# All rows through GpSimd's casting queue: retention followed by a token and channel mixer, on one core

## The chip, the core and the metric

The kernel runs on one core of one Trainium2 chip. The metric is device time in microseconds (us) of one execution, the median of several. A run's state is fast unless it lies over 1.5% above the fastest of the same kernel; only fast runs enter a ratio. A ratio is the mean time of one kernel's fast runs over the mean of the other's fast runs of the same rounds, so it is not quite the ratio of the medians quoted beside it. In the profiles PE is the matrix engine, PEld its weight loads, DVE is VectorE, ACT is ScalarE, POOL is GpSimd and SP is SyncE; each has its own instruction queue.

## The reference

Four batches, eight heads, 768 steps, 64 columns per head. A decayed recurrence over the steps is followed by a mixer over tokens and a mixer over channels (d_tok 256, d_ch 1536):

```python
state = gamma[None, :, None, None] * state + np.einsum('bhd,bhe->bhde', k[:, :, t], v[:, :, t])
y[:, :, t] = scale * np.einsum('bhd,bhde->bhe', q[:, :, t], state)
...
h = np.maximum(xt @ w_tok1, 0.0) @ w_tok2
u = x + h.transpose(0, 2, 1)
h2 = np.maximum(u @ w_ch1, 0.0) @ w_ch2
return (u + h2).astype(np.float32)
```

Inputs and output are f32. The kernel computes in f16 and works in chunks of 128 steps and pairs of heads.

## The kernel before

The kernel doesn't run in the order in which it is written. Every piece of work becomes an `Op` with the engines that may do it and a cost for each. While the program is built, `arrange()` plays the ops through with these costs, picks an engine and a moment for each, and the result is a fixed order for each engine. The plan doesn't exist at run time any more. There, each engine takes its instructions in the planned order and waits at each one for whatever it really depends on. A wrong estimate in the plan therefore never gives a wrong result: it makes an engine stand still at an instruction while others that are ready wait behind it.

For each engine `w[0]` that may do an op, `arrange()` asks when the op could start on it.

```python
for w in op.ways:
    start = max(base, free[w[0]])
    for d in op.deps:
        if d.eng == w[0] and (d.dma or d.eng == "PE"):
            continue
        start = max(start, d.end + (30 if d.eng == w[0] else SEM) + op.guard)
    done = start + w[2] + (300 if w[0] == "DVE" else 0)
    if pick is None or done < pick[0]:
        pick = (done, start, w)
```

For a transfer, `d.end` is the planned landing, worked out by `wires()` from packets and a constant `LAND` per queue. The `continue` skips the wait when the thing waited for was issued by the same engine and is a transfer (`d.dma`).

Rows of k, q and v, for a pair of heads of one batch, come in three ways (cut):

```python
# load(b, p): k and q as f32 by SP's hardware queue, v cast to f16 by GpSimd's software queue
nc.sync.dma_start(out=t, in_=r.rearrange("h (c p) d -> p (h c) d", p=P))        # k, q
nc.gpsimd.dma_start(out=tile_of(s, [P, 2, NC, D], F16), in_=...)                # v
# front(b, p): q is cast and put in the layout of two heads side by side
    ql = parts(emit, dict(POOL=(770, 860), ACT=(780, 860)), [qd], Q, QF, (slice(0, 2),))
# turn(): batches 2 and 3 are transposed by a DMA from SP's queue, batches 0 and 1 by PE
```

`front(b, p)` (recurrence and token mixer of a pair) and `back(b)` (channel mixer of a batch) of different batches interleave. The channel mixer needs no new rows, so it can fill PE while rows come in, if the plan puts it there.

Of the kernel before, what the change touches and what calls it, by code (L numbers as in the profile page):

```python
# [10 lines left out]
FP = mybir.dt.float32  # L11
F16 = mybir.dt.float16
# [5 lines left out]
def kernel(  # L18
# [11 lines left out]
    nc = tc.nc  # L30
    B, H, S, D = q.shape
    P = 128
    NC = S // P
    HC = NC // 2
# [13 lines left out]
    ctx.enter_context(tc.manual_schedule())  # L48


    BUFS = dict(kf=4, qf=4, k16=3, q16=3, v16=6, kT=4, qT=4, U=2, r16=3, am=8, X=3, x16=5, h1=5, u16=3,
                uT=3, h2=2, o=4)
    BANKS = dict(first=range(0, 7), front=range(0, 5), back=range(5, 8), fill=range(7, 8))
    SEM = 80
    XB = 2
# [19 lines left out]
            ops.append(self)  # L75

    GEN = dict(SP=20, ACT=20)
    FIRST = dict(SP=600, POOL=1300, ACT=600)
    LAND = dict(SP=800, POOL=1000, ACT=1500)

    def wires(order):
# [125 lines left out]
    def tile_of(slot, shape, dtype):  # L207
        if slot.bank is not None:
            slot.tile = ps.tile(shape, dtype, name=f"bank{slot.bank}", bufs=1)
        else:  # L210
            slot.tile = sb.tile(shape, dtype, name=slot.tag, bufs=BUFS[slot.tag])
        return slot.tile

    def act(n, scaled=False):
        t = 186 + (93 if scaled else 0) + 5 * n // 6
        return t - 60, t + 20

    def dve(n, per=1.04):
        return int(140 + n * per), int(170 + n * per)
# [4 lines left out]
    def one(eng, cost, emit):  # L224
        return [(eng, cost[0], cost[1], emit)]
# [11 lines left out]
    ident16 = const_p.tile([P, P], F16, name="ident16")  # L237
# [4 lines left out]
    r16 = [const_p.tile([P, NC - 1, P], F16, name=f"r16_{i}") for i in range(NR)]  # L242
# [7 lines left out]
    def emit():  # L250
        nc.gpsimd.iota(itp, pattern=[[0, 1]], base=-MID, channel_multiplier=1,
                       allow_small_or_imprecise_dtypes=True)
# [16 lines left out]
    g_op = prep("ACT", 500, emit, [lgs_op])  # L269

    ident_op = prep("POOL", 560, lambda: make_identity(nc, ident16), prio=(0, -1, 1))
# [11 lines left out]
    wt1 = const_p.tile([P, NC, DT], F16, name="wt1")  # L283
    wt2 = const_p.tile([P, NJ, S], F16, name="wt2")
    NW = 3
    FW = NF // NW
    wc1 = [const_p.tile([P, NP, FW * P], F16, name=f"wc1_{i}") for i in range(NW)]
    wc2 = [const_p.tile([P, FW, C], F16, name=f"wc2_{i}") for i in range(NW)]
    wops = {}
    queue = []  # L290

    def request(prio, cost, emit, dma, takes=()):
        o = Op(prio, [("POOL", cost, cost, emit)], [], takes, dma=dma,
               after=queue[-6:-5], behind=queue[-1] if queue else None)
        queue.append(o)
        return o

    def weight(key, n, ns, dst, src):
        def emit():
            nc.gpsimd.dma_start(out=dst, in_=src.rearrange("(i p) j -> p i j", p=P))  # L300
        wops[key] = request((0, 0, 9), 850, emit, (n, ns))


    casts_of = {(b, p): [] for b in range(B) for p in range(NP)}
# [3 lines left out]
    first_of = {}  # L308
    rcount = [0]

    rows = []

    def load(b, p):
        got = []
        for tag, src in (("kf", k), ("qf", q)):
            s = Slot(tag)

            def emit(s=s, src=src, tag=tag):
                t = tile_of(s, [P, 2, NC, D], FP)
                r = src[b, 2 * p:2 * p + 2]  # L320
                if b < XB and tag == "qf":
                    nc.sync.dma_start(out=t.rearrange("p h (f i) d -> p h f (i d)", f=2),  # L322
                                      in_=r.rearrange("h (f p i) d -> p h f (i d)", f=2, p=P))
                else:
                    nc.sync.dma_start(out=t, in_=r.rearrange("h (c p) d -> p (h c) d", p=P))  # L325
            o = Op((0, b, p), [("SP", 100, 100, emit)], [], [s], dma=(32, 36) if b < XB and tag == "qf" else (96, 17),
                   after=rows[-4:-3], behind=rows[-1] if rows else None)
            rows.append(o)
            got.append((s, o))
        s = Slot("v16")  # L330

        def emit(s=s):
            nc.gpsimd.dma_start(out=tile_of(s, [P, 2, NC, D], F16),  # L333
                                in_=v[b, 2 * p:2 * p + 2].rearrange("h (c p) d -> p (h c) d", p=P))
        got.append((s, request((0, b, p), 1040, emit, (96, 15), [s])))
        loads[b, p] = got

    def front(b, p):
        first, last = b == 0, b == 0 and p == NP - 1
# [3 lines left out]
        def op(ways, deps=(), takes=(), uses=(), late=0, behind=None):  # L343
            n[0] += 1
            pe = ways[0][0] == "PE"
            pr = (late, b, n[0], p) if first else (late, b, p, n[0])
            return Op(pr, ways, deps, takes, uses, guard=200 if pe and not first else 0, behind=behind)

        def parts(emit, costs, deps, slot, src, steps):

            got = []
            for st in steps:
                def put(e, st=st):
                    emit(e, st)
                got.append(op(either(put, **costs), deps, [] if got else [slot],
                              ([slot] if got else []) + [src], behind=got[-1] if got else None))
            return got
# [4 lines left out]
        X, UT = Xs[b], UTs[b]  # L362
        pc = slice(p * P, (p + 1) * P)
        (KF, kd), (QF, qd), (V, vl) = loads[b, p]
        K, Q = Slot("k16"), Slot("q16")
# [5 lines left out]
        def emit(e, js):  # L371
            t = opened(K, [P, NC, 2, D], F16)
            for j in js:
# [2 lines left out]
                    nc.scalar.activation(t[:, :, j], KF.tile[:, j], AF.Copy, scale=gk[:, h:h + 1])  # L376
                else:
                    nc.vector.tensor_scalar(t[:, :, j], KF.tile[:, j], gk[:, h:h + 1], None, ALU.mult)
        kl = parts(emit, dict(ACT=(540, 610), DVE=(490, 540)), [kd, g_op], K, KF, ([0], [1]))

        def emit(e, js):
            t = opened(Q, [P, NC, 2, D], F16).rearrange("p c h d -> p h c d")[:, js]
# [1 line left out]
                nc.scalar.copy(t, QF.tile[:, js])  # L384
            else:
                (nc.vector if e == "DVE" else nc.gpsimd).tensor_copy(t, QF.tile[:, js])  # L386
        if last:
            ql = parts(emit, dict(POOL=(400, 510), ACT=(440, 510), DVE=(490, 540)), [qd], Q, QF,
                       (slice(0, 1), slice(1, 2)))
        elif first:  # L390
            ql = parts(emit, dict(POOL=(770, 860)), [qd], Q, QF, (slice(0, 2),))
        else:
            ql = parts(emit, dict(POOL=(770, 860), ACT=(780, 860)), [qd], Q, QF, (slice(0, 2),))
        casts_of[b, p] += ql

        def flat(t):
            return t.rearrange("p c h d -> p (c h d)")
# [1 line left out]
        def turn(src, dst, dep):  # L399
            if b >= XB:  # L400
                def emit():
                    t = tile_of(dst, [P, S], F16)
                    nc.sync.dma_start_transpose(out=t.rearrange("d (c t) -> d c t", t=P),
                                                in_=flat(src.tile))
                o = Op((0, b, p, 0), [("SP", 100, 100, emit)], dep, [dst], [src], dma=(48, 24))
                return [o, o]
            T = Slot(FA)

            def emit():
                tp = tile_of(T, [P, 1024], F16)  # L410
                for c in range(NC):
                    nc.tensor.transpose(tp[:, c * P:(c + 1) * P], src.tile[:, c].rearrange("p h d -> p (h d)"), ident16)  # L412
            t = op(one("PE", (340, 500), emit), dep + [ident_op], [T], [src])

            def emit(e, hs):
                d, o = opened(dst, [P, S], F16), T.tile[:, :S]
                if dst is QT:
                    d = d.rearrange("d (f p i) -> d f p i", f=2, i=HC)[:, hs]
                    o = o.rearrange("d (f i p) -> d f p i", f=2, i=HC)[:, hs]
                else:  # L420
                    d = d.rearrange("d (f t) -> d f t", f=2)[:, hs]
                    o = o.rearrange("d (f t) -> d f t", f=2)[:, hs]
                (nc.scalar.copy if e == "ACT" else nc.vector.tensor_copy)(d, o)
            per = 1.04 if dst is QT else 0.54
            if last:
                return parts(emit, dict(ACT=act(S // 2), DVE=dve(S // 2, per)), [t], dst, T,
                             (slice(0, 1), slice(1, 2)))
            return 2 * parts(emit, dict(ACT=act(S), DVE=dve(S, per)), [t], dst, T, (slice(0, 2),))
        kt = turn(K, KT, kl)
        qt = turn(Q, QT, ql)  # L430

        two_before = y_done.get(b * NP + p - 2)
        ST, US, RS = Slot(FA), Slot("U"), Slot("r16")
# [277 lines left out]

    for p in range(NP):
        load(0, p)
    weight("t1", 48, 60, wt1, moe_w_tok1)
    weight("t2", 16, 134, wt2, moe_w_tok2)
    for i in range(NW):
        weight(("c1", i), 32, 97, wc1[i], moe_w_ch1[:, i * FW * P:(i + 1) * FW * P])
    for i in range(NW):
        weight(("c2", i), 32, 97, wc2[i], moe_w_ch2[i * FW * P:(i + 1) * FW * P])
    for b in range(1, B):  # L720
        for p in range(NP):
            load(b, p)
# [8 lines left out]
            front(b, p)  # L731
    for b in range(B):
        back(b)
    for key, o in (("t1", casts_of[0, 2][0]), (("c1", 0), casts_of[0, 3][-1])):
        wops[key].deps.append(o)
    best = None
    for turn in range(8):
        order = arrange()
# [50 lines left out]
```

## Time and profile before

216.36 us, median of three runs (215.75 to 217.79). The profiled span is 215.9 us.

| | before |
|---|---|
| PE busy | 199.0 us, of it 12.5 us warm-up on zeros |
| PE not busy (span less busy) | 16.9 us |
| GpSimd busy | 55.9 us |
| DMA engines at 90% or more | until slice 24 of 40, about 130 us |
| last block of PE, two channel mixers without a gap | from 150 us, 62 us long |

A row of the page's second part is read slice by slice: one slice is 5.4 us, a 9 is at least 90% busy. PE is the limit after 130 us and would be before, if rows and what is made of them came in time. The lines themselves stand in the prediction.

### The profile page before, as it was taken

What the parts mean: (1) busy time and instruction counts of PE and PEld (TensorE: products, weight loads), DVE (VectorE), ACT (ScalarE), POOL (GpSimd) and SP (SyncE); (2) the same over time, 40 slices, a digit from 0 to 9 for tenths busy, and PEclk for the clock granted to TensorE, in tenths of its full rate; (3) what the DMA queues carried; (4) which work ended last, traced back from release to release, by engine and by line L of the source; (5) the groups of instructions that cost most, each with busy time, mean ns of one, the idle gap of its engine ahead of it and who ended that gap; (6) DMA issues with size and microseconds to landing.
All of it is one profiled execution on the core that took longest, in us unless ns stands there. A gap on an engine that the chain in (4) does not pass through costs nothing.

```text
span 215.9 us, 4706 instructions
## 1 busy us (share of the span) xinstructions
PE 199.0 (92%) x1893; PEld 123.0 (57%) x1893; DVE 103.7 (48%) x269; ACT 113.1 (52%) x244; POOL 55.9 (26%) x90
## 2 busy tenths in 40 slices
PE   7698799996999999859998699999999999999993
PEld 3465588552367765426665576676645645545541
DVE  6288947402579986118788368874012012012021
ACT  4468996772088964248361677542721712703700
POOL 8225862211016545004332134343000000000000
PEclk9969999999699999999999699999999999999999
DMA  7999999999999999999999998254202112012012
GB/s 156 197 179 263 221 211 219 200 203 181 188 185 226 169 136 162 243 259 173 163 216 159 207 158 165 49 85 108 66 5 105 38 45 101 3 49 99 0 52 99
DMA packets 93207, 30.99 MB, mean 144 GB/s; under 512 B 81920, under 2 KB 90112, under 8 KB 93184
## 3 DMA queue, kind: packets, MB, share of 16 engines
q1 hardware_dynamic: 60672, 17.31, 50.8%
q0 software_dynamic: 29056, 7.08, 35.6%
q10 hardware_dynamic: 3456, 6.29, 8.3%
q8 instruction: 15, 0.25, 0.5%
q14 instruction: 8, 0.07, 0.1%
HBM read 26.74 MB, written 6.29 MB: 153 GB/s over the span
## 4 chain that ended last, share of the span: by engine, by line
PE 69%; DMA 18%; SPq 5%; ACT 3%; DVE 2%; issue 1%; ACTq 0%; POOL 0%
PE bank L695 27%; PE bank L668 25%; DMA v<-in_v_dram 11%; DMA kf<-in_k_dram 5%; PE bank L599 4%; PE bank L548 4%; SPq L322 3%; PE bank L507 2%; PE bank L482 2%; DMA qf<-in_q_dram 2%; PE bank L504 2%; PE bank L439 2%; SPq L325 1%; ACT X L520 1%; DVE am L490 1%; PE bank L412 1%
## 5 line engine op out<-in xcount | busy, mean ns | idle before, releaser
L668 PE MATMUL bank<-uT,wc 128*128 128x384 f16 x384 | 69.4, 327 | 5.0 <-ACT h L682 5.0
L682 ACT ACTIVATE h<-bank 128x384 f16<-128x384 f32 x96 | 46.1, 491 | 49.9 <-DVE o L703 24.0
L695 PE MATMUL bank<-wc,h 128*128 128x512 f16 x288 | 69.3, 386 | 0.1
L668 PEld LDWEIGHTS <-wc 128*128 128x128 f16 x384 | 35.7, 98 | 27.9 <-issue 5.8
L703 DVE TENSOR_TENSOR o<-X,bank 128x512 f32<-128x512 f32 x24 | 16.5, 688 | 62.0 <-PE bank L695 61.9
L695 PEld LDWEIGHTS <-h 128*128 128x128 f16 x288 | 26.9, 99 | 29.1 <-issue 2.0
L490 DVE TENSOR_TENSOR am<-bank,mask 128x384 f16<-128x384 f32 x64 | 32.1, 550 | 21.4 <-PE bank L482 21.3
L333 POOL DMA_DIRECT2D v<-in_v_dram x16 | 16.7, 1043 | 20.9 <-PE bank L507 10.9
L520 ACT ACTIVATE X<-bank,gy 128x192 f32<-128x192 f32 x50 | 18.0, 419 | 7.1 <-PE bank L507 6.9
L537 POOL CAST x<-X 128x384 f16<-128x384 f32 x23 | 12.0, 521 | 30.2 <-ACT X L520 16.4
L607 DVE TENSOR_TENSOR X<-X,bank 128x384 f32<-128x384 f32 x32 | 16.3, 550 | 5.8 <-PE bank L599 5.4
L615 POOL CAST u<-X 128x384 f16<-128x384 f32 x23 | 11.3, 509 | 28.7 <-DVE X L607 25.6
L451 DVE SCALAR_TENSOR_TENSOR U<-U,gp,bank 128x64 f32<-128x64 f32 x64 | 17.8, 278 | 1.5
L507 PE MATMUL bank<-v,am 128*128 128x64 f16 x192 | 15.0, 197 | 0.5 <-DVE am L490 0.4
L376 ACT ACTIVATE k<-kf,gk 128x384 f16<-128x384 f32 x22 | 12.8, 609 | 3.4 <-DMA kf<-in_k_dram 3.3
L599 PE MATMUL bank<-h,wt 128*128 128x128 f16 x192 | 14.0, 225 | 0.7 <-ACT h L556 0.7
L507 PEld LDWEIGHTS <-am 128*128 128x128 f16 x192 | 12.9, 101 | 2.8 <-DVE am L490 0.8
L462 ACT ACTIVATE r<-U 64x320 f16<-64x320 f32 x26 | 12.1, 467 | 3.5 <-DVE U L451 3.1
L599 PEld LDWEIGHTS <-wt 128*128 128x128 f16 x192 | 12.2, 101 | 2.8 <-issue 0.9
L386 POOL CAST q<-qf 128x768 f16<-128x768 f32 (+1 forms) x12 | 9.8, 815 | 15.2 <-DMA qf<-in_q_dram 15.2
L756 PE MATMUL bank<-zero 128*128 128x384 f16 x53 | 12.5, 382 | 1.2 <-DVE zero L248 1.2
L548 PE MATMUL bank<-x,wt 128*128 128x128 f16 x192 | 13.4, 219 | 0.2 <-DMA wt<-in_moe_w_tok_dram 0.2
(56 smaller groups left out, 154.0 us busy)
## 6 DMA issues: line engine op xcount, KB each, us to landing
kf<-in_k_dram SPq DMA_DIRECT2D x16, 384.0 KB, 9.3
qf<-in_q_dram SPq DMA_DIRECT2D x16, 384.0 KB, 9.8
out_dram<-o ACTq DMA_DIRECT2D x24, 256.0 KB, 2.0
v<-in_v_dram POOLq DMA_DIRECT2D x16, 192.0 KB, 14.6
wc<-in_moe_w_ch_dram POOLq DMA_DIRECT2D x6, 512.0 KB, 16.5
wt<-in_moe_w_tok_dram POOLq DMA_DIRECT2D x2, 384.0 KB, 7.6
kT<-k SPq DMA_TRANSPOSE x8, 6.1
qT<-q SPq DMA_TRANSPOSE x8, 6.2
```

What stands on the lines that cost most here:

```text
L333: nc.gpsimd.dma_start(out=tile_of(s, [P, 2, NC, D], F16), in_=v[b, 2 * p:2 * p + 2].rearrange("h (c p) d -> p (h c) d", p=P))
L451: nc.vector.scalar_tensor_tensor(U[:, c], U[:, c - 1], gp[:, p:p + 1], o, ALU.mult, ALU.add)
L490: nc.vector.tensor_tensor(am, src, m, ALU.mult)
L507: nc.tensor.matmul(o[:, j * D:(j + 1) * D], AM[2 * hf + j].tile[:, i], V.tile[:, j, c], start=(c == 0), stop=(c == 0 or j == 1))
L520: nc.scalar.mul(X.tile[:, half(hf), h * D:(h + 1) * D], yv[:, :, j * D:(j + 1) * D], gy[:, h:h + 1])
L548: nc.tensor.matmul(acc[:, jt * P:(jt + 1) * P], wt1[:, i, jt * P:(jt + 1) * P], X16.tile[:, i], start=(i == 0), stop=(i == NC - 1))
L599: nc.tensor.matmul(acc[:, i * P:(i + 1) * P], wt2[:, jt, t], H1.tile[:, jt], start=(jt == 0), stop=(jt == NJ - 1))
L607: nc.vector.tensor_tensor(xo, xo, T2.tile[:, :HC * P].rearrange("p (i d) -> p i d", d=P), ALU.add)
L668: nc.tensor.matmul(acc[:, :SH], w[:, ct, (ft % FW) * P:(ft % FW + 1) * P], UT.tile[:, ct, sh * SH:(sh + 1) * SH], start=(ct == 0), stop=(c ...
L682: nc.scalar.activation(H2.tile[:, ft], A.tile[:, :SH], AF.Relu)
L695: nc.tensor.matmul(A.tile, H2.tile[:, ft, i * P:(i + 1) * P], wc2[ft // FW][:, ft % FW], start=(ft == 0), stop=(ft == NF - 1))
L703: nc.vector.tensor_tensor(o, X.tile[:, sh * HC + i], A.tile, ALU.add)
```

## The change

The intent: let the casting queue of GpSimd bring all rows as f16, so that the f32 casts of q go away and SP's queue is free for transposes; order that queue as it is needed (rows of the first batch, weights, the rest); and for batches 0 and 1 let PE turn q straight from the loaded tile, one head at a time, so that q isn't copied there at all. In batches 2 and 3 q is still copied into the layout of two heads, now from f16 to f16, and VectorE is added to the engines that may do it.

```diff
-    BUFS = dict(kf=4, qf=4, k16=3, q16=3, v16=6, ...
+    BUFS = dict(kf=6, qf=6, k16=3, q16=3, v16=8, ...
-    FIRST = dict(SP=600, POOL=1300, ACT=600)
+    FIRST = dict(SP=600, POOL=1700, ACT=600)
...
-               after=queue[-6:-5], behind=queue[-1] if queue else None)
+               after=queue[-8:-7], behind=queue[-1] if queue else None)
...
-        for tag, src in (("kf", k), ("qf", q)):
+        for tag, src in (("kf", k), ("qf", q), ("v16", v)):
...
+            def emit(s=s, src=src):
+                nc.gpsimd.dma_start(out=tile_of(s, [P, 2, NC, D], F16),
+                                    in_=src[b, 2 * p:2 * p + 2].rearrange("h (c p) d -> p (h c) d", p=P))
...
-        else:
-            ql = parts(emit, dict(POOL=(770, 860), ACT=(780, 860)), [qd], Q, QF, (slice(0, 2),))
+        if b < XB:
+            ql = [qd]
+        else:
+            ql = parts(emit, dict(POOL=(770, 860), ACT=(780, 860), DVE=(500, 550)), [qd], Q, QF, (slice(0, 2),))
...
+                    if src is QF:
+                        for j in range(2):
+                            nc.tensor.transpose(o[j * D:(j + 1) * D], src.tile[:, j, c], ident16)
```

Cut: costs of single ops in the plan, the place of the first two requests in its order, the waits of two weight requests for casts that no longer exist, and the plain eviction of the turned q, which the new layout allows.

More of the change, by code (lines that the diff above doesn't have):

```diff
@@ L48 @@
     ctx.enter_context(tc.manual_schedule())
-    BUFS = dict(kf=4, qf=4, k16=3, q16=3, v16=6, kT=4, qT=4, U=2, r16=3, am=8, X=3, x16=5, h1=5, u16=3,
+    BUFS = dict(kf=6, qf=6, k16=3, q16=3, v16=8, kT=4, qT=4, U=2, r16=3, am=8, X=3, x16=5, h1=5, u16=3,
                 uT=3, h2=2, o=4)
@@ L309 @@
     rcount = [0]
-    rows = []
     def load(b, p):
         got = []
-        for tag, src in (("kf", k), ("qf", q)):
+        for tag, src in (("kf", k), ("qf", q), ("v16", v)):
             s = Slot(tag)
-            def emit(s=s, src=src, tag=tag):
-                t = tile_of(s, [P, 2, NC, D], FP)
-                r = src[b, 2 * p:2 * p + 2]
-                if b < XB and tag == "qf":
-                    nc.sync.dma_start(out=t.rearrange("p h (f i) d -> p h f (i d)", f=2),
-                                      in_=r.rearrange("h (f p i) d -> p h f (i d)", f=2, p=P))
-                else:
-                    nc.sync.dma_start(out=t, in_=r.rearrange("h (c p) d -> p (h c) d", p=P))
-            o = Op((0, b, p), [("SP", 100, 100, emit)], [], [s], dma=(32, 36) if b < XB and tag == "qf" else (96, 17),
-                   after=rows[-4:-3], behind=rows[-1] if rows else None)
-            rows.append(o)
-            got.append((s, o))
-        s = Slot("v16")
-        def emit(s=s):
-            nc.gpsimd.dma_start(out=tile_of(s, [P, 2, NC, D], F16),
-                                in_=v[b, 2 * p:2 * p + 2].rearrange("h (c p) d -> p (h c) d", p=P))
-        got.append((s, request((0, b, p), 1040, emit, (96, 15), [s])))
+            def emit(s=s, src=src):
+                nc.gpsimd.dma_start(out=tile_of(s, [P, 2, NC, D], F16),
+                                    in_=src[b, 2 * p:2 * p + 2].rearrange("h (c p) d -> p (h c) d", p=P))
+            pr = (0, -1, 0) if (b, p) == (0, 0) and tag != "v16" else (0, b, p)
+            got.append((s, request(pr, 1040, emit, (96, 14.5), [s])))
         loads[b, p] = got
@@ L378, in emit @@
                     nc.vector.tensor_scalar(t[:, :, j], KF.tile[:, j], gk[:, h:h + 1], None, ALU.mult)
-        kl = parts(emit, dict(ACT=(540, 610), DVE=(490, 540)), [kd, g_op], K, KF, ([0], [1]))
+        kl = parts(emit, dict(ACT=(540, 610), DVE=(410, 465)), [kd, g_op], K, KF, ([0], [1]))
         def emit(e, js):
@@ L386, in emit @@
                 (nc.vector if e == "DVE" else nc.gpsimd).tensor_copy(t, QF.tile[:, js])
-        if last:
-            ql = parts(emit, dict(POOL=(400, 510), ACT=(440, 510), DVE=(490, 540)), [qd], Q, QF,
-                       (slice(0, 1), slice(1, 2)))
-        elif first:
-            ql = parts(emit, dict(POOL=(770, 860)), [qd], Q, QF, (slice(0, 2),))
-        else:
-            ql = parts(emit, dict(POOL=(770, 860), ACT=(780, 860)), [qd], Q, QF, (slice(0, 2),))
-        casts_of[b, p] += ql
+        if b < XB:
+            ql = [qd]
+        else:
+            ql = parts(emit, dict(POOL=(770, 860), ACT=(780, 860), DVE=(500, 550)), [qd], Q, QF, (slice(0, 2),))
         def flat(t):
@@ L411, in emit @@
                 for c in range(NC):
-                    nc.tensor.transpose(tp[:, c * P:(c + 1) * P], src.tile[:, c].rearrange("p h d -> p (h d)"), ident16)
-            t = op(one("PE", (340, 500), emit), dep + [ident_op], [T], [src])
+                    o = tp[:, c * P:(c + 1) * P]
+                    if src is QF:
+                        for j in range(2):
+                            nc.tensor.transpose(o[j * D:(j + 1) * D], src.tile[:, j, c], ident16)
+                    else:
+                        nc.tensor.transpose(o, src.tile[:, c].rearrange("p h d -> p (h d)"), ident16)
+            t = op(one("PE", (600, 760) if src is QF else (340, 500), emit), dep + [ident_op], [T], [src])
             def emit(e, hs):
                 d, o = opened(dst, [P, S], F16), T.tile[:, :S]
-                if dst is QT:
-                    d = d.rearrange("d (f p i) -> d f p i", f=2, i=HC)[:, hs]
-                    o = o.rearrange("d (f i p) -> d f p i", f=2, i=HC)[:, hs]
-                else:
-                    d = d.rearrange("d (f t) -> d f t", f=2)[:, hs]
-                    o = o.rearrange("d (f t) -> d f t", f=2)[:, hs]
+                d = d.rearrange("d (f t) -> d f t", f=2)[:, hs]
+                o = o.rearrange("d (f t) -> d f t", f=2)[:, hs]
                 (nc.scalar.copy if e == "ACT" else nc.vector.tensor_copy)(d, o)
-            per = 1.04 if dst is QT else 0.54
             if last:
-                return parts(emit, dict(ACT=act(S // 2), DVE=dve(S // 2, per)), [t], dst, T,
+                return parts(emit, dict(ACT=act(S // 2), DVE=dve(S // 2, 0.54)), [t], dst, T,
                              (slice(0, 1), slice(1, 2)))
-            return 2 * parts(emit, dict(ACT=act(S), DVE=dve(S, per)), [t], dst, T, (slice(0, 2),))
+            return 2 * parts(emit, dict(ACT=act(S), DVE=dve(S, 0.54)), [t], dst, T, (slice(0, 2),))
         kt = turn(K, KT, kl)
-        qt = turn(Q, QT, ql)
+        qt = turn(QF if b < XB else Q, QT, ql)
         two_before = y_done.get(b * NP + p - 2)
@@ L713 @@
         load(0, p)
-    weight("t1", 48, 60, wt1, moe_w_tok1)
-    weight("t2", 16, 134, wt2, moe_w_tok2)
+    weight("t1", 48, 50, wt1, moe_w_tok1)
+    weight("t2", 16, 118, wt2, moe_w_tok2)
     for i in range(NW):
-        weight(("c1", i), 32, 97, wc1[i], moe_w_ch1[:, i * FW * P:(i + 1) * FW * P])
+        weight(("c1", i), 32, 80, wc1[i], moe_w_ch1[:, i * FW * P:(i + 1) * FW * P])
     for i in range(NW):
-        weight(("c2", i), 32, 97, wc2[i], moe_w_ch2[i * FW * P:(i + 1) * FW * P])
+        weight(("c2", i), 32, 80, wc2[i], moe_w_ch2[i * FW * P:(i + 1) * FW * P])
     for b in range(1, B):
@@ L733 @@
         back(b)
-    for key, o in (("t1", casts_of[0, 2][0]), (("c1", 0), casts_of[0, 3][-1])):
-        wops[key].deps.append(o)
     best = None
```

## The prediction

> **What bounds the kernel now.** I read the page first: busy times, slices, chain.
>
> ```profile
> PE 199.0 (92%) x1893; PEld 123.0 (57%) x1893; DVE 103.7 (48%) x269; ACT 113.1 (52%) x244; POOL 55.9 (26%) x90
> ...
> DMA  7999999999999999999999998254202112012012
> ...
> PE 69%; DMA 18%; SPq 5%; ACT 3%; DVE 2%; issue 1%; ACTq 0%; POOL 0%
> ```
>
> PE is busy 92% of the span and carries 69% of the chain that ended last; the DMA engines are at 90% or more until slice 24 (about 130 us), then nearly free. So there are two limits in turn: the supply of rows early, PE afterwards. Some of PE's work is no work: the group of warm-up matmuls on `zero` (L756) is 12.5 us, all in the first 24 us. Real PE work is about 199.0 - 12.5 = 186.5 us, so the 216 us hold about 29 us that a better supply could touch.
>
> Next I read PE's timeline and waits for where they lie. The first batch ends when its last operands come: k and q of pair 3 land late (the last k is scaled at 21.56, the last q is cast at 23.36), then w_tok1 is waited for at 26.06. From there PE is nearly solid except for these:
>
> ```profile
> PE bank L668 <- ACT h L682: 5.0, 2, 3.2
> PE bank L439 <- DMA v<-in_v_dram: 4.2, 2, 2.3
> ...
> PE bank L599 <- ACT h L556: 0.7, 1, 0.7
> ```
>
> (engine, line and what it waited for: us in total, times, longest.) The two v waits are 1.9 us near 9.97 and 2.33 us at 54.42. The two L668 waits are 3.16 us before 94.35 and 1.88 us before 119.99. The chain of waits shows what was behind two of these:
>
> ```profile
> 29.98 24.40 DMA v<-in_v_dram
> 54.42 0.35 PE bank L439 x10
> ...
> 87.70 1.01 SPq L403
> 88.81 4.52 DMA qf<-in_q_dram
> 93.41 0.35 ACTq L709
> ```
>
> v of batch 1, pair 0 took 24.4 us from issue to landing: its request stood behind six requests for w_ch1 and w_ch2 in the software queue. At 88.81 a q of a later batch was only just being issued by SP, behind a DMA transpose that had held SP's queue for 4.95 us. ACT, in order, stood behind that. The third wait lies where rows are still arriving (the last k request leaves at 117.3, the last q request at 121.4). After 26.06 the gaps are 2.33 + 3.16 + 1.88 + 0.67 = 8.0 us, plus the last add and store (212.3 to 215.9, 3.6 us). The two last batches are one solid PE block from 150 to 212 us, which no supply can shorten.
>
> **What the Trainium skill says.** "DMA: Bandwidth & Descriptors", section "Issuing engines are not separate DMA queues": queues of different engines run on the same 16 DMA engines and interleave, so using more of them saves only issue time. The trace agrees, and more: counted from its packet records, one DMA engine moves 53 packets in a us while SP's queue of 256 B rows is alone, up to 68 while the software queue's casting rows are almost alone (14.7 ns each), but 26 + 26 when both run (19.2 ns each). Section "SWDGE vs HWDGE vs iDMA" of that page: a cast needs the software queue, whose descriptors GpSimd writes. That is the 1.02 us of GpSimd per v request here. "SBUF — State Buffer", section "Who interferes with whom": a VectorE copy in a two-port mode shuts GpSimd out, so such a queue can starve. The 16 v requests took 1.009 to 1.251 us, median 1.016, so before it hardly happens. "TensorE: Matmul & The Clock Gate", section "Back-to-back issue gap" (with the phases above it): 128 columns cost about 55.6 ns at full clock. The trace agrees: six transposes of q from 36.95 leave PE to the next group at 37.28, 55 ns each.
>
> **The change part by part.**
>
> *Rows by one casting queue.* SP loses 32 row requests and keeps only transposes; GpSimd gets 32 more at 1.02 us, +32.6 us. It loses the q casts of batches 0 and 1 (some 0.83 us each where they were GpSimd's: about six, -5 us). 55.9 + 32.6 - 5 = 83 us of GpSimd, most of it in the first 120 us: loaded, not full. Bytes read are unchanged; what is written halves. DMA-engine time for rows: 48 requests x 96 packets per engine x 14.7 ns = 68 us. Before, taken at the rates of a queue alone (16 k and 8 q x 96 x about 17 ns = 39 us, 8 q x 32 x 36 ns = 9 us, 16 v x 96 x 14.7 ns = 23 us) it is 71 us, and more while queues mix. So the volume is hardly a saving; the order and the free SP queue are.
>
> *Start-up.* The software queue starts later: v of pair 0 was issued at 1.53 and its packets began near 4.5 us, SP's first k was issued at 0.81 and began near 2.0. With the first request at about 1.0 I put the first packets at 4.0. Twelve requests x 96 x 14.7 ns = 16.9 us: rows are in at 20.9 on a middling engine and about 22.5 on the slowest (before, the last q landed at 20.7 on the middling and 22.6 on the slowest engine, 10% longer over the same stretch). In queue order the third-last and second-last requests, k and q of pair 3, land near 20 and 21.5, where before they were 21.5 and 22.6 with a 0.51 us cast still to come; but v of pair 3 now lands last (22.5 to 23, before 20.8). Its states, five VectorE steps of 0.28 us and two scalings of 0.48, then still follow. w_tok1: 48 x 50 ns = 2.4 us behind the rows, so about 25.5 on the slowest engine, before 26.06. Worth at the start of dense PE work: about 1 us, not more.
>
> *Weights behind the rows, batch 1 behind the weights.* Tok weights 4.3 us, six channel weights x 32 packets x about 85 ns (10 packets in a us, beside 9 rows) = 16.3 us. They end near 41.5, batch 1's first k, q and v by 46.5, slowest engine perhaps 48. Before, that v came at 54.4. The 2.33 us wait should go. The last rows of batch 1 come near 59, before at 65.8. From there 24 requests x 1.41 us = 34 us and half of the transposes (12 k and q and u of batch 2 x 48 packets x about 21 ns = 12 us) put the last row near 105 to 110 instead of about 126. The waits at 94 and 120, 5.0 us, and most of the 0.67 should go, since a q request no longer stands behind a transpose. Expected of the 8.0 us: all but leftovers.
>
> *q by head.* Each pair of batches 0 and 1 has 12 transposes instead of 6: 6 x 55 ns = 0.33 us. The four of batch 0 lie among warm-up matmuls and cost nothing; the four of batch 1 lie in dense PE time: +1.3 us. Evictions of q become contiguous, k scalings on VectorE read f16 (0.41 us now): not on PE's path.
>
> *New waits.* The orders of all engines come out anew from the plan, and a static order that is a little wrong costs PE a gap somewhere. GpSimd must issue in order between casts of x and u for which PE waits. I allow 2.5 us.
>
> Sum: 216.4 - 1 - 8 + 1.3 + 2.5 = 211.2. A part of the half-clock dip at 55 us (0.66 for 5 us, after PE had idled) may go along with the gap that preceded it, 0 to 1.7 us; half of it, 0.8: **210.4 us**.
>
> **Rivals.** (1) *GpSimd becomes the bound.* For: 32 more requests, a slot wait of one holds up everything behind it; before, GpSimd already waited 10.9 us for PE L507 ahead of v requests. Against: its share was 26% and becomes some 40%. If x and u casts come 1 us late in each of 12 later fronts and a third shows on PE, +4: 214 to 216. (2) *The straggling engine.* With all rows in one queue every pair waits for the slowest of 16 engines; v of batch 2 landed 3 to 6 us behind the middling engine (the first: 64.9 median, 70.8 last). If that persists without SP's competing rows, batch 0 ends 2 us later than before and the 54 us gap halves: 213 to 215. (3) *Supply was hidden anyway and VectorE and ACT bound the mixed stage.* Between 62 and 90 us PE is busy 27.96 of 28 us while VectorE has 21.85 and ACT 19.60; faster rows then merely move waits. For: from 15 to 30 us both were busy about 13 of 15. Then only the 54 and 94 us gaps go: 212 to 213. (4) *Better than summed.* If smoother supply also shortens the first batch, because VectorE and ACT begin the late pairs earlier and are not crowded after 20 us, dense PE starts 3 us sooner: 207.
>
> **Range and chances.** Floor: 26.06 - 3, plus 177.9 us of real PE work and 3.6 us of tail (215.9 - 26.06 - 8.0 - 3.6 = 178.2, same thing within rounding), plus 1.3: about 206. Rival 1 or 2 in full gives 215. So 206.3 to 214.8 should hold it 8 times in 10. The line for 2% is 212.0; my sum lies 1.6 below it with a spread of about 3.3: faster 0.66, same 0.29, slower 0.05. Slower needs rivals 1 and 2 together.
>
> **What would show it.** Right: the waits of PE for v at 54 us and for ACT h at 94 us are gone; SP issues only transposes; first v of batch 1 lands by 48 us; DMA falls below 90% some 15 us earlier, near slice 21; L412 for q has 96 + 0 matmuls in place of 48, by head; the solid L668/L695 block starts about 145 instead of 150 us and lasts 62 us again. Wrong on start-up: w_tok1's first matmul (L548) after 27 us. Wrong on GpSimd: its casts (x, u) and not PE or ACT head the releasers of PE waits, or its DMA issues last well over 1.02 us. Wrong on supply: row requests still land 15 us after issue and PE waits for L439 between 45 and 100 us.

## The result, and the profile after

The changed kernel took 238.06 us (236.29 to 239.78, four runs) against 216.97 us for the kernel before in the same rounds: ratio 1.0977, 95% interval 1.0864 to 1.1089. It is 10% slower. The forecast was faster, 206.3 to 214.8 us.

Busy times, slices and chain of the changed kernel's page, after the clock row of the kernel before:

```profile
PEclk9969999999699999999999699999999999999999
```

```profile
PE 205.1 (87%) x1938; PEld 124.6 (53%) x1938; DVE 102.4 (44%) x274; ACT 107.8 (46%) x237; POOL 82.6 (35%) x116
...
PEclk9999999999559965996799999999999999999999
DMA  8999999999699699999889895312121202102112
...
PE 62%; DMA 21%; POOL 7%; issue 5%; DVE 2%; ACT 1%; SPq 1%; POOLq 0%; ACTq 0%
```

The span is 18.7 us longer (234.6 - 215.9). PE is not busy for 29.5 us instead of 16.9, which is 12.6 of them; it is busy for 205.1 us instead of 199.0, which is the other 6.1. The row of PEclk shows why busy time grew: before it has single sixes, here there are three stretches of 5 to 7. The trace's clock records give 10.2, 10.2 and 6.8 us at half clock, 27.3 us, against three times 3.4 us before. Half clock for 17 us more would lose 8.5 us of PE time; it is less because PE stood still in a part of them. Each stretch begins 2 to 5 us after the start of a gap of PE. GpSimd is at 7% on the chain (0% before); SP's queue, 5% before, is nearly gone from it, as intended.

Where the time went is plain from one stretch of 50 us, in the view of busy times by stretch (PE, PEld, DVE, ACT and POOL busy with counts, then granted clock, DMA share, GB/s; the share sums the times of packets that overlap, so it can exceed 1, and bytes count as written). First before, then after:

```profile
60.00:110.00 50.00, 46.80 (x544) 30.90 (x543) 33.59 (x85) 31.99 (x71) 18.88 (x28) 1.00 1.56 194
```

```profile
60.00:110.00 50.00, 34.35 (x353) 21.68 (x353) 21.80 (x60) 19.19 (x43) 26.09 (x33) 0.77 1.35 110
```

All engines but GpSimd do a third less, at 0.77 of the clock, and the DMA engines move 110 GB/s instead of 194. A part of that last drop is no loss, since rows written as f16 count half as much (e9_pair_land9 below moves 159). Nothing is full; everything waits. For what, the waits of PE say, and then those of GpSimd (engine and line, what it waited for: us in total, times, longest):

```profile
PE bank L529 <- POOL x L518: 15.9, 5, 6.3
PE bank L463 <- DMA kT<-k: 4.7, 3, 3.3
```

```profile
POOL q L371 <- DMA qf<-in_q_dram: 28.3, 5, 9.8
...
POOL q L371 <- issue: 11.0, 3, 5.8
```

PE waits 15.9 us for x, which GpSimd casts in 0.51 us each. GpSimd doesn't cast it because it stands at L371, the f16 copy of q, for 39.3 us in all (28.3 + 11.0; "issue" is a wait whose releaser the profile doesn't name, here at the same instruction). All eight copies of q of batches 2 and 3 are on GpSimd. The chain of waits shows the first of them:

```profile
49.40 10.80 DMA qf<-in_q_dram
60.20 0.05 issue
60.26 0.28 POOL q L371
...
62.02 0.52 POOL x L518
62.54 0.95 POOL kf L317
63.49 0.45 POOL x L518
63.93 5.58 DMA qf<-in_q_dram
```

GpSimd issues the request for q of batch 2, pair 0 at 49.40. The next instruction in its queue is the copy of that same q. Seven earlier requests of the software queue have not landed at that time, and it lands 10.8 us later. Until then GpSimd does nothing else: not the casts of x of batch 1, of which ACT had made the first ready by 54 us (four evictions to X from 52.62) and which PE lacks from 56.3, and not the next requests, so that the DMA engines run dry at about 59 us. It then makes the copy, casts two pieces of x, issues three requests, the last at 63.93 for the next q, and stands again, 4.62 us, until that q has landed 5.58 us after its request. Each stand delays the requests behind it too: the last row lands at 138.4 us, against 128.2 in the kernel before and 111.0 in e1_rule below, where GpSimd doesn't stand at q.

Why would a tuned plan put a copy right behind its own load? The plan, printed while the kernel is built, says (us; the landing is the plan's own):

```
q of batch 2, pair 0: request 49.3, landing 63.1, copy on GpSimd 50.4
q of batch 2, pair 1: request 54.9, landing 68.6, copy on GpSimd 55.9
q of batch 2, pair 2: request 60.3, landing 74.0, copy on GpSimd 61.4
q of batch 2, pair 3: request 65.2, landing 80.8, copy on GpSimd 66.3
q of batch 3, pair 0: request 69.9, landing 91.8, copy on GpSimd 70.9
```

It plans every copy before its own data are there, the other three too. That is the rule in `arrange()` shown above: a dependency on a transfer of the same engine is skipped. Before, it never applied to a copy, because SP issued q and GpSimd cast it. The kernel before with this rule restricted to transfers compiles to the same instructions, on every engine (built, not run). With the change, request and copy are on GpSimd, the rule applies, and GpSimd even looks like the best place for the copy, as it is the one engine on which q seems to be there at once. The plan's own end, printed at building too, gives no warning: it is 203.2 us for the kernel before, 203.3 for the change, 203.3 for e1_rule and 202.4 for e9_pair_land9.

The early part went as hoped: the first w_tok1 matmul begins at 24.64 us (26.06 before), the first v of batch 1 lands at 44.9 us (54.4 before), and PE has no gap of more than 0.3 us from 23 to 56 us.

### The profile page after: what moved, and what is told of

The parts are those of the page before. It is cut to its first block, busy times and chain, and to the rows that moved or that the text cites. A ratio compares the mean times of both kernels' runs of the same rounds, so it can differ in the third digit from the quotient of the medians.

```text
span 234.6 us, 4770 instructions
## 1 busy us (share of the span) xinstructions
PE 205.1 (87%) x1938; PEld 124.6 (53%) x1938; DVE 102.4 (44%) x274; ACT 107.8 (46%) x237; POOL 82.6 (35%) x116
## 4 chain that ended last, share of the span: by engine, by line
PE 62%; DMA 21%; POOL 7%; issue 5%; DVE 2%; ACT 1%; SPq 1%; POOLq 0%; ACTq 0%
PE bank L649 25%; PE bank L676 22%; DMA qf<-in_q_dram 10%; DMA kT<-k 8%; PE bank L580 4%; DMA kf<-in_k_dram 3%; PE bank L529 3%; POOL kf L317 2%; PE bank L463 2%; POOL v L317 1%; PE bank L488 1%; POOL qf L317 1%; PE bank L485 1%; PE bank L551 1%; POOL q L371 1%
## 5 line engine op out<-in xcount | busy, mean ns | idle before, releaser
L471 DVE TENSOR_TENSOR am<-bank,mask 128x384 f16<-128x384 f32 x64 | 34.2, 550 | 13.5 <-PE bank L463 13.1
L529 PE MATMUL bank<-x,wt 128*128 128x128 f16 x192 | 15.3, 232 | 16.0 <-POOL x L518 15.9
L529 PEld LDWEIGHTS <-wt 128*128 128x128 f16 x192 | 13.2, 104 | 18.6 <-issue 17.0
L371 POOL COPY q<-qf 128x768 f16<-128x768 f16 x8 | 6.6, 827 | 39.3 <-DMA qf<-in_q_dram 28.3
L518 POOL CAST x<-X 128x384 f16<-128x384 f32 x28 | 13.9, 512 | 15.7 <-ACT X L501 9.7
L537 ACT ACTIVATE h<-bank 128x256 f16<-128x256 f32 x14 | 5.4, 384 | 27.6 <-PE bank L529 27.6
L317 POOL DMA_DIRECT2D kf<-in_k_dram x16 | 16.5, 1031 | 4.2 <-DMA wc<-in_moe_w_ch_dram 2.2
L317 POOL DMA_DIRECT2D qf<-in_q_dram x16 | 16.4, 1022 | 3.8 <-DMA wc<-in_moe_w_ch_dram 1.8
L361 ACT ACTIVATE k<-kf,gk 128x384 f16<-128x384 f16 x22 | 12.7, 609 | 7.6 <-DMA kf<-in_k_dram 5.7
L443 ACT ACTIVATE r<-U 64x320 f16<-64x320 f32 x30 | 13.8, 465 | 5.3 <-DVE U L432 4.9
L463 PE MATMUL bank<-qT,kT 64*128 64x128 f16 x192 | 10.5, 231 | 5.0 <-DMA kT<-k 4.7
```

Of the source, the lines that this page charges most:

```text
L463: nc.tensor.matmul(a[j][:, i], KT.tile[r, t], QT.tile[r, t], start=True, stop=True)
L471: nc.vector.tensor_tensor(am, src, m, ALU.mult)
L529: nc.tensor.matmul(acc[:, jt * P:(jt + 1) * P], wt1[:, i, jt * P:(jt + 1) * P], X16.tile[:, i], start=(i == 0), stop=(i == NC - 1))
```

## The experiments

The theory (A) is the one just told. Its rivals: (B) GpSimd or its queue can't carry 48 row requests; (C) turning q by head costs PE more than thought. Eleven kernels ran; all were correct. Beside each time stands the median of the kernel before in the same rounds.

### e1_rule: the plan counts the landing

```diff
-    if d.eng == w[0] and (d.dma or d.eng == "PE"):
+    if d.eng == w[0] and (d.dma and op.dma or d.eng == "PE"):
```

> Theory A (the planner lets a GpSimd copy of q follow its own GpSimd request at once, because it skips the wait for a transfer of the same engine; on the chip GpSimd then stands still until q lands): with that one rule limited to transfers that wait for transfers, all 16 requests of batches 2 and 3 and their casts remain, but GpSimd's waits for q (39.3 us in the changed kernel) fall below 5 us, PE's waits for x from GpSimd (15.9 us) below 3 us, the half-clock stretches shrink to about 10 us, and the time is 207 to 213 us. Theory B (GpSimd is overloaded by 32 more requests, or the casting queue is too slow): requests and bytes are the same as in the changed kernel, so 230 us or more. Theory C (q by head on PE and its clock): by head is unchanged, so at least 225 us.

Measured: 217.49 us against 217.35, ratio 1.0023 (0.998 to 1.0065). 48 row requests, casts and by-head transposes are all still there (four of the eight copies of q still on GpSimd, now after their landings), and 20.6 of the 21.1 us of loss are gone. GpSimd waits for no q any more and PE not for x. B and C fall as causes of the slowdown. But the time isn't 207 to 213 us either: the forecast for the change as meant is still missed by 7 us. PE's waits in this kernel:

```profile
PE bank L463 <- DMA qT<-q: 6.3, 2, 5.1
PE bank L463 <- DMA kT<-k: 3.4, 1, 3.4
```

PE now waits 9.7 us for DMA transposes of q and k, which were the smaller item (4.7 us) in the changed kernel.

### e2_not_pool: GpSimd may not copy q

```diff
-    ql = parts(emit, dict(POOL=(770, 860), ACT=(780, 860), DVE=(500, 550)), ...
+    ql = parts(emit, dict(ACT=(780, 860), DVE=(500, 550)), ...
```

> The rule of the planner is left as it is in the changed kernel; only GpSimd is taken away from the engines that may copy q of batches 2 and 3 (ACT or VectorE do it, and for those the planner does count the landing). Theory A: the same cure by another way, 207 to 214 us, no wait of GpSimd for q. Theory B and C: 225 us or more, since queue, requests and transposes are unchanged.

Measured: 218.89 us against 217.35, ratio 1.0042 (0.9969 to 1.0115). The same cure by another way, and the same result: the loss goes, the gain doesn't come, and the 207 to 214 us that I gave are missed by 5. PE's waits again name the transposes (this profile fell in the run counted as slow, 219.5 us, so it is only read for what was waited for):

```profile
PE bank L463 <- DMA qT<-q: 12.0, 5, 6.0
```

### e3_half: GpSimd may copy q of batch 3 only

```diff
+    ways = dict(ACT=(780, 860), DVE=(500, 550)) if b == XB else \
+        dict(POOL=(770, 860), ACT=(780, 860), DVE=(500, 550))
```

> The planner's rule as in the changed kernel; GpSimd may copy q of batch 3 but not of batch 2. Theory A: four blind waits instead of eight. The first four cost GpSimd 24 us of the 39 and lie where PE had its gaps of 6.3, 1.0, 1.2, 3.6 and 3.3 us, so less than half of the loss should remain: 213 to 223 us, and GpSimd waits for q of 8 to 25 us, all after the plan's batch 3. Theory B and C: 225 us or more.

Measured: 231.98 us against 217.35, ratio 1.0685 (1.0619 to 1.0751). GpSimd's waits for q:

```profile
POOL q L371 <- DMA qf<-in_q_dram: 18.5, 3, 7.6
...
POOL q L371 <- issue: 3.9, 1, 3.9
```

The waits are as expected (22.4 us, 57% of 39.3), the time is not. I expected less than half of the loss to remain; 14.5 of 20.6 us (231.98 and 238.06 less e1_rule's 217.49) do, 70%. So fewer blind waits lose less, but not in proportion, and the later four were not the cheap ones. PE waits for x only 4.0 us here, and for transposes 11.1 us; but the row requests still come late, the last row landing at 131.3 us (138.4 with eight blind waits, 111.0 with none). That this makes up the rest is not shown by itself.

### e5_rule_pair: e1_rule, q of batches 0 and 1 by pair again

```diff
-        if b < XB:
-            ql = [qd]
-        else:
+        if True:
...
-        qt = turn(QF if b < XB else Q, QT, ql)
+        qt = turn(Q, QT, ql)
```

> As e1_rule, but q of batches 0 and 1 is copied into the two-head layout again and turned by pair (6 transposes instead of 12), so the by-head part of the change is undone. By head costs PE 6 x 55 ns more for each of 4 pairs in dense time, 1.3 us; undoing it gives that back but puts eight more copies of 0.5 to 0.8 us on ACT, VectorE or GpSimd in crowded stretches. Within 2 us of e1_rule either way; I expect 0 to 2 us slower. If by head were what costs (theory C), it would be over 4 us faster than e1_rule.

Measured: 214.97 us against 217.35, ratio 0.9907 (0.9846 to 0.9968). Undoing the by-head part is 2.5 us faster, not 0 to 2 us slower; it is not the over 4 us that would have made it the cause.

### e6_rule_land: e1_rule, and transposes land later in the plan

The plan lets a DMA transpose of e1_rule land 3.8 us after issue (median). On the chip those issued from 63 to 84 us, while rows were moving, took 7.9 to 11.4 us, and those after 110 us, when rows were nearly done, mostly 2.8. Before, SP's queue held f32 rows too, and the plan had put landings of transposes at 12.6 us (median of all 24; 13.8 for q and k) where the chip took 2.8 to 11.4 for q and k: mostly too long, and PE never waited there.

```diff
-    LAND = dict(SP=800, POOL=1000, ACT=1500)
+    LAND = dict(SP=5300, POOL=1000, ACT=1500)
```

> As e1_rule, and the planner adds 5.3 us instead of 0.8 us to the landing of whatever SP issues (transposes only). In e1_rule the plan had a DMA transpose land 3.8 us after issue (median), the chip took 7 to 11 us while rows were moving, and PE waited 9.7 us for them in scores (L463); before, the plan had said 12.6 us. Theory D (what e1_rule still lacks against the forecast of 210.4 is this mistaken landing): PE's waits for qT and kT fall from 9.7 us below 3 us, the half-clock stretch after them goes (6.8 us at half speed, worth 3.4), and the time is 207 to 212 us. Theory E (rows and transposes crowd the DMA engines, so PE must idle there whatever the order): 215 to 218 us, PE's waits merely move.

Measured: 210.23 us against 216.28, ratio 0.9715 (0.9671 to 0.976). Faster, and at the forecast of the change. The transposes don't land sooner (q and k: 9.2 us, median); PE merely does other work meanwhile. Its waits for them are now:

```profile
PE bank L463 <- DMA qT<-q: 2.3, 4, 0.9
...
PE bank L463 <- DMA kT<-k: 1.4, 1, 1.4
```

Theory D holds and E falls: the crowding of DMA engines is real, but the order of PE's work decides whether it costs anything. At 3.7 us the waits are a little above the 3 us named.

### e8_rule_shallow: e1_rule with the row buffers of before

```diff
-    BUFS = dict(kf=6, qf=6, k16=3, q16=3, v16=8, ...
+    BUFS = dict(kf=4, qf=4, k16=3, q16=3, v16=6, ...
```

> As e1_rule with the row buffers of the kernel before (4 for k, 4 for q, 6 for v instead of 6, 6, 8), the plan's landings unchanged. Theory E: fewer rows in flight, transposes land sooner, PE's waits for them fall below 6 us and the time is 2 us or more below e1_rule. Theory D: landings stay far above the plan's 3.8 us, PE still waits 7 us or more, 215 to 219 us.

Measured: 220.87 us against 216.28, ratio 1.0198 (1.0152 to 1.0244), which is unclear at 2%. PE still waits 9.7 us for transposes (8.2 and 1.5). Fewer rows in flight don't cure it. The time is 2 us above what I gave. In the profile PE idles as long as in e1_rule from the first w_tok1 matmul to its last (9.7 us in both) and is busy 2.4 us longer, with 10.2 us at half clock against 6.8, which can make up to 1.7 of that.

### e7_pair_land and e9_pair_land9: both cures, q by pair

```diff
 e7_pair_land:  e6_rule_land with the edit of e5_rule_pair
 e9_pair_land9: the same with LAND = dict(SP=9000, ...)
```

> As e6_rule_land with q of batches 0 and 1 turned by pair (as e5_rule_pair). Theory D: e5_rule_pair's waits for qT (5.9 us) go too: 207 to 211 us, 1 to 3 us below e6_rule_land as e5_rule_pair was 2.5 us below e1_rule. Theory E: as e5_rule_pair, 214 to 216 us.

> As e7_pair_land with 9.0 us instead of 5.3 us added to SP's landings (the plan then says 11.8 us, near the 12.6 us of the kernel before). Theory D: no wait of PE for a transpose at all, and within 2 us of e7_pair_land: what the last gap gives, later fronts may take. Theory E: 214 us or more.

Measured: 207.98 us, ratio 0.9598 (0.9529 to 0.9666), and 204.78 us, ratio 0.9453 (0.9415 to 0.9491), against 216.28 us. e9_pair_land9 beats both kernels: 5.5% faster than before. It lies 3.2 us from e7_pair_land, a little more than the 2 us expected, and on the good side. Its page:

```profile
PE 194.4 (96%) x1887; PEld 119.5 (59%) x1887; DVE 108.2 (53%) x284; ACT 109.3 (54%) x234; POOL 81.1 (40%) x113
...
PEclk9999999999999999999999999999999999999999
```

and the same 50 us of it:

```profile
60.00:110.00 50.00, 50.00 (x617) 33.30 (x617) 41.95 (x106) 33.50 (x76) 30.63 (x42) 1.00 1.87 159
```

PE is busy in all of them, no wait for a transpose is left, and the clock never falls before the end. GpSimd issues all 48 row requests and is busier in this stretch (30.63 us) than in the changed kernel (26.09 us): it was never too slow, it stood still. The DMA engines move 159 GB/s, less than the 194 of before, since half of each row's written bytes are gone.

### e10_land_only: the second cure without the first

```diff
-    LAND = dict(SP=800, POOL=1000, ACT=1500)
+    LAND = dict(SP=9000, POOL=1000, ACT=1500)
```

> The changed kernel with 9.0 us added to SP's landings in the plan and its rule for waits left alone: the second cure without the first. The plan still puts all eight copies of q on GpSimd, five of them 1 us behind their own request. Theory A: GpSimd stands still as in the changed kernel (over 20 us for q in all) and the time is 222 to 238 us, far from the 204.8 us that both cures together gave. If the landing of transposes were the whole matter: 205 to 212 us.

Measured: 223.41 us against 217.09, ratio 1.031 (1.0248 to 1.0372). All eight copies are on GpSimd still, and its waits for q are 34.1 us:

```profile
POOL q L371 <- DMA qf<-in_q_dram: 24.9, 5, 9.8
...
POOL q L371 <- issue: 9.2, 2, 5.5
```

The rule is needed. The two faults also make each other worse, as e11_rule_land9 below, with neither, shows: the rule alone costs 223.41 - 209.69 = 13.7 us, the landing alone 217.49 - 209.69 = 7.8 us, both together 238.06 - 209.69 = 28.4 us, more than the sum of 21.5. That a plan with later landings has more other work on PE while GpSimd is stuck would explain it, but no run shows that by itself.

### e11_rule_land9: e9_pair_land9 with q by head

```diff
 e1_rule with LAND = dict(SP=9000, ...)
```

> As e9_pair_land9, but q of batches 0 and 1 by head as in the changed kernel. Both pairs so far put by head at +2.3 to 2.5 us (217.5 to 215.0, 210.2 to 208.0), the working from PE alone at +1.3 us. I expect 206 to 208 us, 1.3 to 2.5 us above e9_pair_land9, with the solid last block of PE beginning that much later.

Measured: 209.69 us against 217.09, ratio 0.9649 (0.9585 to 0.9713), 4.9 us above e9_pair_land9: a miss (206 to 208). By head is slower in all three pairs of runs, by 2.5, 2.3 and 4.9 us (4.2 by the ratios in the last pair, which ran in different rounds). The added transposes explain little of it. In the changed kernel's timeline twelve transposes by head begin at 44.98 and the next matmul at 45.44, 0.46 us, where six by pair before them take 0.34 us (44.12 to 44.46); four pairs of batch 1 make 0.5 us of that, not 1.3. In e11_rule_land9 PE has one gap of 2.5 us at 112 us, for a transpose, and a half clock of 3.4 us after it; e9_pair_land9 has neither. In all three pairs most of the rest is a later start and waits: the first w_tok1 matmul begins 0.4, 1.1 and 0.2 us later by head, and from there to its last matmul PE idles 9.7, 3.8 and 2.5 us by head, 6.1, 2.6 and 0.0 us by pair. Whether the plan's order for by-head kernels is merely less lucky or by head makes it so stays open.

### e12_pair_land14: more margin

```diff
 e9_pair_land9 with LAND = dict(SP=14000, ...)
```

> As e9_pair_land9 with 14 us instead of 9. In e9_pair_land9 PE waits for no transpose any more, so more margin has nothing to remove: 204 to 208 us, no better by more than 0.5 us, worse if later fronts run out of time.

Measured: 212.8 us against 217.09, ratio 0.979 (0.9737 to 0.9844), unclear at 2%, and a miss by 5 us. PE's longest gap is a wait of 6.2 us for an eviction of ACT:

```profile
PE bank L483 <- ACT X L499: 6.2, 1, 6.2
```

ACT's timeline shows where it is from:

```profile
108.03 0.61 ACT L361 ACTIVATE k<-kf,gk 128x384 f16<-128x384 f16 x1 [7.09 <-DMA kf<-in_k_dram]
108.55 0.71 ACT L499 ACTIVATE X<-bank,gy 128x192 f32<-128x192 f32 x2
```

ACT stood 7.09 us at a scaling of k whose row hadn't landed, and the eviction behind it (L499), for which PE waited, came late. It is the same picture on a third engine: a landing misjudged, and an in-order queue stuck at it. A margin on one kind of transfer moves the other work of the plan too, so more of it isn't safer. One constant changed from 9 to 14 us moved the time by 7 to 8 us; some of what e6_rule_land and e9_pair_land9 gain may thus be where their order happened to fall, and no run separates that.

The main kernels at a glance (idle is span less PE busy of the profiled run; half clock from the clock records, before PE's last matmul):

| kernel | us | ratio to before | PE idle, us | half clock, us |
|---|---|---|---|---|
| before | 216.97 | 1 | 16.9 | 10.2 |
| the change | 238.06 | 1.0977 | 29.5 | 27.3 |
| e1_rule | 217.49 | 1.0023 | 17.4 | 6.8 |
| e6_rule_land | 210.23 | 0.9715 | 12.2 | 0 |
| e9_pair_land9 | 204.78 | 0.9453 | 8.9 | 0 |

## Why the prediction was wrong, point by point

**What bounds the kernel: right.** PE's gaps were worth having. In e9_pair_land9 PE doesn't stop between the first w_tok1 matmul (24.54 us) and its last matmul (199.59), the time falls to 204.8 us, and the last matmul of a front ends at 141 us instead of 150. My floor of about 206 was a little high: its 177.9 us of PE work held two stretches at half clock; in e9_pair_land9, without them, it is 175.1.

**Rows by one casting queue, start-up, batch 1 behind the weights: right, sizes a little off.** One DMA engine moves 75.5 row packets in a us with the software queue alone, 13.2 ns each instead of my 14.7. I had misread the trace: the kernel before already reaches 73 in one us (from 54.3), where I wrote "up to 68". For SP's rows I also put 17 ns where my own 53 packets in a us make 18.9; no term of the sum rests on it. First packets came at 3.3 us (4.0 predicted), the last row of batch 0 at 21.8 (22.5 to 23), the first w_tok1 matmul at 24.64 (about 1 us earlier than before; it was 1.4), the first v of batch 1 at 44.9 (46.5 to 48), its last row at 57.7 (59). The waits for v at 54 us are gone. The last row, forecast for 105 to 110 us, landed at 138.4, but at 111.0 in e1_rule, where DMA also falls below 90% after slice 21, as forecast: the supply was judged well and lost to the standing still.

**"*New waits.* ... I allow 2.5 us": the step that failed.** I wrote there that "GpSimd must issue in order between casts of x and u for which PE waits", and in rival 1 that one wait of GpSimd holds up everything behind it, worth 4 us. That part came: PE's waits are headed by GpSimd's casts of x (15.9 us), the sign that I had named for "Wrong on GpSimd". What held GpSimd up, a copy standing behind its own request, was not in it, and so the size failed: 39.3 us of waits at eight copies, 20.6 us of the time by e1_rule. I took the waits for scatter of a plan that is "a little wrong" and did not ask what the plan does with the moved instructions. It could have been read: the diff puts request and copy of q on one engine, and the fourth line of the rule says that such a wait isn't counted. GpSimd's load was forecast well, 83 us against 82.6; the sum counted what the remaining copies take (0.83 us each) and had no term for what they wait, behind a queue seven requests deep.

**"The waits at 94 and 120 ... should go, since a q request no longer stands behind a transpose": half right.** They went, and transposes took their place: 9.7 us of PE's waits in e1_rule, where I had counted 5.0 us as gained and 2.5 us for all new waits. Freeing SP's queue took the f32 rows out of it, and with them the overlong landings that had given the plan its margin. This is the term that separates e1_rule's 217.5 from the forecast of 210.4; with 4.5 us of margin back, e6_rule_land gives 210.2. That it meets my number is partly chance, since by head and the start were each off in their own way.

**"*q by head* ... +1.3 us": wrong size.** PE pays 0.5 us for it in dense time; the time pays 2.3 to 4.9 us, mostly in waits and a later start, whose cause isn't settled.

**Rivals.** Rival 1 named the right engine for the wrong reason: load. Rival 2, the slowest DMA engine, didn't matter: the last row of batch 0 landed at 20.5 on the middling and 21.8 us on the slowest engine. Rivals 3 and 4 forecast gains, and the changed kernel has none. "Slower: 0.05" rested on rivals 1 and 2 alone.

## What to carry to other kernels

Before moving a load to another engine, look at what follows it in that engine's queue: an in-order engine that issues a transfer and then uses it stands still for the whole landing, with everything else behind it. "DMA: Bandwidth & Descriptors" of the Trainium skill, section "Rules for kernel authors", says to issue early and wait late; this puts 20 us on it. And where a planner fixes the order, compare its landings with the trace's after each change of queues, because a rule or a constant that was harmless for one queue can fail, unseen, on another.

## What the Trainium skill lacked or had wrong

- "DMA: Bandwidth & Descriptors" gives first-byte latencies of about 1 us for the software queue and 0.6 us for the hardware queues. Here the first packet began 1.9 us after GpSimd's first request began to issue (1.41 to 3.29) in the changed kernel and 3.1 us after (1.53 to 4.61) in the kernel before; SP's took 1.1 us (0.81 to 1.93).
- The same page says that queues of several engines interleave and that this only saves issue time. No page says what mixing costs: with 256 B rows, one DMA engine moves 75.5 packets per us for the casting queue alone (309 GB/s read over 16 engines) and 53 for SP's alone (kernel before, 92 to 94 us). Taken by turns at these rates it would be an estimated 31 + 31; it was 26 + 26.
- No page gives the landing time of a DMA transpose beside other traffic: 2.8 us when rows were done, 7.9 to 11.4 us while the casting queue was full (e1_rule, 128 x 768 f16).
- "TensorE: Matmul & The Clock Gate" says that gaps over some 3.4 us lower PE's clock (section "HAM oscillation"). In the kernel before a gap of 2.33 us at 52.1 us was followed by 3.4 us at half clock, and one of 3.16 us at 91.2 us by none; in e1_rule one of 3.44 us at 70.0 us was followed by none either. So the length of one gap alone doesn't tell.
